# Linear attention followed by a gated feed-forward block: new row layout, k maximum as a factor on v, new load order

## The chip, the cores and the metric

The kernel runs on one core of one Trainium2 chip. The metric is the time of one execution in microseconds (us) on the device. A run counts as slow when it is over 1.5% above the fastest of the same kernel.

The engines in the profile: PE is the tensor engine, PEld its weight loads, DVE the vector engine, ACT the scalar engine, POOL the GpSimd engine, SP the sync engine. SPq and POOLq mark the issuing of DMA transfers. PSUM is the memory that the matmuls of these kernels write to, SBUF the one that holds all other tiles. The buffers of a tile in a pool are called its ring. L230 is line 230 of the kernel in question, so the same work has different line numbers in different kernels.

## The reference

```python
# q, k, v: (8, 8, 576, 64) = batch, head, row, feature; omega: (128, 64)
def phi(x):                                    # x = q * scale or k * scale
    proj = einsum('bhsd,md->bhsm', x, omega)
    h = proj - sum(x * x, -1, keepdims) / 2
    h = h - max(h, -1, keepdims)
    return exp(h) / sqrt(m)
kv  = einsum('bhsm,bhsd->bhmd', k_p, v);  z = sum(k_p, axis=2)
num = einsum('bhsm,bhmd->bhsd', q_p, kv); den = einsum('bhsm,bhm->bhs', q_p, z) + 1e-6
x   = (num / den) as (4608, 512)               # 8 heads side by side
out = (gelu(x @ w_gate) * (x @ w_val)) @ w_out # (512, 1536), (512, 1536), (1536, 512)
```

Factors that are constant in a row of q cancel in num / den, so the kernel needs no maximum for q (the 1e-6 aside). For k, exp(proj − max) can be written as exp(proj) · exp(−max): the second factor belongs to a row of k and may as well be multiplied onto that row of v (and onto the 1 that sums up z).

## The kernel before

A *batch* is one of the 8 batch entries, with 576 tokens. The FFN works on 9 tiles of 512 tokens. Attention for batch t+1 is woven into the FFN of tile t, so that the tensor engine fills the waits of attention with FFN matmuls. For batches 2 to 7, k and q are transposed by DMA, and so is the attention's result x; batches 0 and 1 use the tensor engine for it.

```python
SM = 512; R = 4; SR = S - SM        # rows 0..511 of a head: s = 4p + r; 64 rows left over
work = ctx.enter_context(tc.tile_pool(name="work", bufs=2))
att  = ctx.enter_context(tc.tile_pool(name="att", bufs=2, space=PSUM))
mo   = ctx.enter_context(tc.tile_pool(name="mo", bufs=4, space=PSUM))
# ... loads: k, q of a batch in three pieces each on the GpSimd queue, v in three on the sync queue ...
def k_feat(ps, dst, n):             # for each PSUM tile of keys
    nmax = work.tile([P, n, 1], F32, name="nmax", bufs=4)
    nc.vector.reduce_max(nmax, ps, axis=AX, negate=True)
    kd = work.tile([P, n, M], F32, name="kd", bufs=5)
    nc.vector.tensor_add(kd, ps, nmax.broadcast_to((P, n, M)))
    nc.scalar.activation(dst, kd, func=Exp)
# ... pk in four tiles and a left-over one; q features; kz = k_p^T [v, 1] ...
for rp in range(2):
    x_sb = work.tile([P, 2, d_model], BF16, name="x_sb")       # the pool's 2 buffers
    for r2 in range(2):
        nd = att_tile([P, 2, 512], F32, "nd")
        # ... 8 matmuls into nd, reciprocal of the denominators ...
        nc.vector.tensor_mul(x_sb[:, r2]..., ndv[:, :, :, :D], iden.broadcast_to(...))
    if on_dma:                                                 # batches 2 to 7
        for r2 in range(2):
            put_x_dma(tok + (2 * rp + r2) * P, x_sb[:, r2], P) # DMA transposes x_sb -> xT
        continue
# ... the 64 left-over rows go another way, through PSUM ...
def gate_val(t):
    for jf in range(N_DFF):                                    # 12 times
        g_ps = mo.tile([P, T_TOK], F32, name="g_ps", tag="mo") # 4 matmuls of 512 columns
        nc.scalar.activation(g_gelu, g_ps, func=Gelu)
        v_ps = mo.tile([P, T_TOK], F32, name="v_ps", tag="mo") # 4 matmuls
        nc.vector.tensor_mul(gated[:, jf, :], g_gelu, v_ps)
```

The softmax here doesn't subtract the row's maximum and nothing guards it: scores larger than these inputs give would overflow.

Of the kernel before, what the change touches and what calls it, by code (L numbers as in the profile page):

```python
# [10 lines left out]
F32 = mybir.dt.float32  # L11
# [4 lines left out]
def kernel(  # L16
# [29 lines left out]
    SM = 512  # L46
    R = 4
    SR = S - SM
# [5 lines left out]
    AX = mybir.AxisListType.X  # L54

# [8 lines left out]


    def load_kq(b):
        tiles = []
        for src, nm in ((k, "k"), (q, "q")):
            both = ld.tile([P, 2 * H + 2, P], BF16, name=f"{nm}_in")
            main = both[:, :2 * H].rearrange("p (h c) x -> p h (c x)", h=H)  # L70
            rest = both[:, 2 * H:].rearrange("p c (j d) -> p (c j) d", j=2)
            nc.gpsimd.dma_start(  # L72
                out=main,
                in_=src[b, :, :SM, :].rearrange("h (p r) d -> p h (r d)", r=R))
            for e in range(2):
                hs = src[b].rearrange("(j e) s d -> e j s d", e=2)[e] if nm == "k" \
                    else src[b, 4 * e:4 * e + 4]
                nc.gpsimd.dma_start(
                    out=rest[e * SR:(e + 1) * SR],
                    in_=hs[:, SM:, :].rearrange("j s d -> s j d"))  # L80
            tiles += [both, main, rest]
        return tiles

    v_ext = [singles.tile([P, H, R, DP1], BF16, name=f"v_ext{i}") for i in range(2)]

    v_rbd = [singles.tile([P, 4, 2, DP1], BF16, name=f"v_rbd{i}") for i in range(2)]

    for i in range(2):
        nc.vector.memset(v_rbd[i], 0.0)
        nc.vector.memset(v_ext[i][:, :, :, D:DP1], 1.0)  # L90
        for e in range(2):
            nc.vector.memset(v_rbd[i][e * SR:(e + 1) * SR, :, e, D:DP1], 1.0)

    def load_v(b):
        vf = ld.tile([P, H, R * D], F32, name="vf", bufs=1)
        vrf = ld.tile([P, 4, D], F32, name="vrf", bufs=1)
        nc.sync.dma_start(
            out=vf, in_=v[b, :, :SM, :].rearrange("h (p r) d -> p h (r d)", r=R))
        for e in range(2):
            nc.sync.dma_start(  # L100
                out=vrf[e * SR:(e + 1) * SR],
                in_=v[b].rearrange("(j e) s d -> e j s d", e=2)[e, :, SM:, :]
                    .rearrange("j s d -> s j d"))
        ve, vr = v_ext[b % 2], v_rbd[b % 2]
        nc.gpsimd.tensor_copy(ve[:, :, :, :D],
                              vf.rearrange("p h (r d) -> p h r d", r=R))
        for e in range(2):
            sl = slice(e * SR, (e + 1) * SR)
            nc.gpsimd.tensor_copy(vr[sl, :, e, :D], vrf[sl])
        return ve, vr  # L110

    omega_f = singles.tile([M, D], F32)
    nc.sync.dma_start(out=omega_f, in_=omega)
    kq = {0: load_kq(0)}
    vx = {0: load_v(0)}

    ident = singles.tile([P, P], BF16)
    make_identity(nc, ident)
    omega_bf = singles.tile([M, D], BF16)
    nc.vector.tensor_scalar_mul(omega_bf, omega_f, scale)  # L120
    omegaT_ps = att_tile([D, M], BF16, "omegaT_ps")
    nc.tensor.transpose(omegaT_ps, omega_bf, ident)
    omegaT2 = singles.tile([2 * D, M], BF16)
    omega2T = singles.tile([2 * D, 2 * M], BF16)
    nc.vector.memset(omega2T, 0.0)
    for e in range(2):
        sl = slice(e * D, (e + 1) * D)
        nc.vector.tensor_copy(omegaT2[sl], omegaT_ps)
        nc.vector.tensor_copy(omega2T[sl, e * M:(e + 1) * M], omegaT_ps)
# [12 lines left out]

    load_gv(0)
    kq[1] = load_kq(1)
    vx[1] = load_v(1)
    load_gv(1)
    load_gv(2)
    for c in range(3):
        nc.gpsimd.dma_start(out=w_out_sb[:, 4 * c:4 * c + 4, :], in_=wo[:, 4 * c:4 * c + 4, :])


    x_tiles = {}

    def put_x(c0, src):

        n, done = src.shape[2], 0
        while done < n:
            t, c = divmod(c0 + done, T_TOK)
            m = min(n - done, T_TOK - c)
            if t not in x_tiles:  # L160
                x_tiles[t] = work.tile([P, N_DM, T_TOK], BF16, name="xT", bufs=3)
            nc.vector.tensor_copy(x_tiles[t][:, :, c:c + m], src[:, :, done:done + m])
            done += m

    def put_x_dma(c0, src, n):

        done = 0
        while done < n:
            t, c = divmod(c0 + done, T_TOK)
            m = min(n - done, T_TOK - c)  # L170
            if t not in x_tiles:
                x_tiles[t] = work.tile([P, N_DM, T_TOK], BF16, name="xT", bufs=3)
            nc.sync.dma_start_transpose(out=x_tiles[t][:, :, c:c + m],
                                        in_=src[done:done + m, :])
            done += m


    def transpose_dma(both, nm):
        t_sb = work.tile([P, 2 * H + 2, P], BF16, name=f"{nm}T", tag="kqT")
        nc.sync.dma_start_transpose(out=t_sb, in_=both.rearrange("p c x -> p (c x)"))  # L180
        return t_sb

    def transpose_main(src, nm):
        t_ps = att_tile([P, 2 * H, P], BF16, f"{nm}T_ps")
        for h in range(H):
            for rp in range(2):
                nc.tensor.transpose(t_ps[:, 2 * h + rp, :],  # L187
                                    src[:, h, rp * P:(rp + 1) * P], ident)
        t_sb = work.tile([P, 2 * H + 2, P], BF16, name=f"{nm}T", tag="kqT")[:, :2 * H]
        nc.vector.tensor_copy(t_sb, t_ps)  # L190
        return t_sb

    def attention(b):
        k_both, k_in, k_rest, q_both, q_in, q_rest = kq.pop(b)
        ve, vr = vx.pop(b)
        on_dma = b > 1
        if on_dma:
            kT = transpose_dma(k_both, "k")
            qT = transpose_dma(q_both, "q")
            krT, qrT = kT[:, 2 * H:], qT[:, 2 * H:]  # L200
        else:
            kT = transpose_main(k_in, "k")
            rT_ps = att_tile([P, 4, P], BF16, "rT_ps")
            for i, src in enumerate((k_rest, q_rest)):
                for jj in range(2):
                    nc.tensor.transpose(
                        rT_ps[:, 2 * i + jj, :],
                        src[:, 2 * jj:2 * jj + 2, :].rearrange("p j d -> p (j d)"), ident)
            rT = work.tile([P, 4, P], BF16, name="rT")
            nc.vector.tensor_copy(rT, rT_ps)  # L210
            krT, qrT = rT[:, :2], rT[:, 2:]


        k_p = work.tile([P, H, R, M], BF16, name="k_p")
        k_pr = work.tile([P, 4, M], BF16, name="k_pr")

        def k_feat(ps, dst, n):
            nmax = work.tile([P, n, 1], F32, name="nmax", bufs=4)
            nc.vector.reduce_max(nmax, ps, axis=AX, negate=True)  # L219
            kd = work.tile([P, n, M], F32, name="kd", bufs=5)  # L220
            nc.vector.tensor_add(kd, ps, nmax.broadcast_to((P, n, M)))  # L221
            nc.scalar.activation(dst, kd, func=Exp)  # L222

        for hp in range(H // 2):
            pk = att_tile([P, 8, M], F32, "pk")
            for i in range(4):
                nc.tensor.matmul(pk[:, 2 * i:2 * i + 2, :], kT[:, 4 * hp + i, :], omega2T)  # L227
            k_feat(pk, k_p[:, 2 * hp:2 * hp + 2].rearrange("p h r m -> p (h r) m"), 8)
        pkr = att_tile([P, 4, M], F32, "pkr")
        for jj in range(2):  # L230
            nc.tensor.matmul(pkr[:, 2 * jj:2 * jj + 2, :], krT[:, jj, :], omega2T)
        k_feat(pkr, k_pr, 4)


        if not on_dma:
            qT = transpose_main(q_in, "q")
        q_pT = work.tile([P, H // 2, 2, 4, P], BF16, name="q_pT")
        q_pTr = work.tile([P, 2, 2, P], BF16, name="q_pTr")
        for hp in range(H // 2):
            pq = att_tile([P, 2, 512], F32, "pq")  # L240
            for r2 in range(2):
                sl = slice(r2 * D, (r2 + 1) * D)
                nc.tensor.matmul(pq[:, r2, :], omegaT2[sl],  # L243
                                 qT[sl, 4 * hp:4 * hp + 4, :])
            nc.scalar.activation(  # L245
                q_pT[:, hp].rearrange("m a c p -> m a (c p)"), pq, func=Exp)
        pqr = att_tile([P, 2, 512], F32, "pqr")
        for j2 in range(2):
            sl = slice(j2 * D, (j2 + 1) * D)
            nc.tensor.matmul(pqr[:, j2, :256], omegaT2[sl], qrT[sl])  # L250
        nc.scalar.activation(q_pTr.rearrange("m a c p -> m a (c p)"), pqr[:, :, :256], func=Exp)


# [152 lines left out]
```

## Time and profile before

| what | value |
|---|---|
| median of 3 runs | 399.51 us (398.19 to 399.78) |
| profiled span | 398.3 us, mean granted clock 0.977 |
| PE / DVE / ACT / POOL busy | 355.4 / 224.2 / 154.6 / 63.0 us |
| start of the stage of batch 2 | 91.65 us |
| one stage from there (one batch's attention with one tile's FFN) | 38.2 us four times and 38.4 once; then 115.4 us to the end |

The start of a stage is read from the scalar engine. Exp and Gelu use different tables, and the timeline shows each change of table (1.28 us); the change to Exp (L222 before) stands right before a batch's first exponentials of k. I use these moments as stage marks.

The page's slices of the kernel before (40 equal slices; each digit is the busy share in tenths, or the granted clock in tenths) with the chain that ended last (by engine):

```profile
PE   0446756999999999999999999999999999999995
PEclk9999985899999999999999999999999999999999
PE 80%; DVE 9%; DMA 4%; issue 2%; ACT 2%; POOL 1%; SPq 0%; DVEq 0%; POOLq 0%
```

PE is half idle in the first 70 us and busy at 90% or more from then on. The busy table of one stage (window, its length, then busy time and instruction count of each engine, granted clock, DMA share, GB/s) says the same by number:

```profile
91.65:129.84 38.19, 37.98 (x247) 18.07 (x250) 25.05 (x38) 18.73 (x24) 6.99 (x9) 1.00 0.79 135
```

PE is busy 37.98 of 38.19 us at full clock, DVE only 25.05. In the start, the timeline of the first keys shows a chain on DVE (start, duration, engine, line, instruction; in brackets the idle time before it and what ended it):

```profile
17.34 1.91 PE L227 MATMUL pk<-omega2T,kT 128*128 128x256 bf16 x8
18.44 2.36 DVE L219 TENSOR_REDUCE nmax<-pk 128x8 f32<-128x1024 f32 x2 [0.43 <-PE pk L227]
20.71 2.35 DVE L221 TENSOR_TENSOR kd<-pk,nmax 128x1024 f32<-128x1024 f32 x2
...
21.99 2.17 PE L227 MATMUL pk<-omega2T,kT 128*128 128x256 bf16 x8 [2.73 <-DVE kd L221]
```

Two key tiles take two maxima and two adds, 4.7 us in all, and PE reuses the first one's PSUM tile only after its add, at 21.99. The last view of before is of the tile `x_sb` in one stage.

```profile
L281 DVE TENSOR_TENSOR x_sb<-nd,iden x4: 680/688/692, 111.1 to 113.8; 128x512 bf16<-128x512 f32 x4
L173 SPq DMA_TRANSPOSE xT<-x_sb x4: 1226/1332/1455, 119.3 to 123.6; - x4
DMA to landing us min/median/max: 5.9/7.2/7.6
```

The four products are written from 111.1 to 113.8 us. Their transposes are issued only from 119.3 to 123.6, and land 5.9 to 7.6 us after issue. They are late, and nothing waits for them here.

### The profile page before, as it was taken

The page shows a single profiled execution, that of the slowest core. Times are in us where ns is not written, and L with a number is a line of the kernel's source. Part 1 is how long each engine was busy: PE and PEld are TensorE (multiplying, and loading weights), DVE is VectorE, ACT ScalarE, POOL GpSimd, SP SyncE. Part 2 cuts the span into 40 slices and gives each one's busy share as a digit, 9 for nine tenths or more (in the row PEclk, how much of TensorE's full clock was granted, in tenths as well). Part 3 has the DMA queues.
Part 4 walks back from the last instruction along what each step waited for, and adds up shares of the span by engine and source line. Part 5 has one row for each costly group of instructions (what it writes and reads, how often), then busy time and mean ns, then how long its engine had stood idle before and what let it go on. Part 6 is the DMA issues. An engine that isn't in the chain of part 4 may idle for free.

```text
span 398.3 us, 5658 instructions
## 1 busy us (share of the span) xinstructions
PE 355.4 (89%) x2212; PEld 174.2 (44%) x2249; DVE 224.2 (56%) x345; ACT 154.6 (39%) x202; POOL 63.0 (16%) x87
## 2 busy tenths in 40 slices
PE   0446756999999999999999999999999999999995
PEld 0323523545444544444444444454535444444442
DVE  1392593748574956495559546864776423433332
ACT  1044027234833482447335633653464312311310
POOL 7563422600222041104100200000000000000000
PEclk9999985899999999999999999999999999999999
DMA  9999999980799089909992820371022012002004
GB/s 179 234 213 219 206 232 154 192 157 0 142 158 209 8 144 225 150 11 189 167 150 47 185 49 1 70 176 35 0 88 58 16 33 72 2 27 81 0 10 95
DMA packets 89626, 43.65 MB, mean 110 GB/s; under 512 B 55808, under 2 KB 84992, under 8 KB 89600
## 3 DMA queue, kind: packets, MB, share of 16 engines
q1 hardware_dynamic: 59504, 29.14, 34.2%
q0 software_dynamic: 30096, 14.16, 28.1%
q8 instruction: 17, 0.28, 0.3%
q14 instruction: 9, 0.07, 0.1%
HBM read 37.78 MB, written 9.44 MB: 119 GB/s over the span
## 4 chain that ended last, share of the span: by engine, by line
PE 80%; DVE 9%; DMA 4%; issue 2%; ACT 2%; POOL 1%; SPq 0%; DVEq 0%; POOLq 0%
PE g_ps L327 23%; PE v_ps L333 23%; PE o_ps L357 21%; DVE nmax L219 3%; DMA q_in<-in_q_dram 3%; DVE kd L221 3%; PE pk L227 3%; PE nd L276 2%; PE kz_ps L261 2%; PE pq L243 2%; ACT q_pT L245 2%; DMA out_dram<-o_sb 1%; PE qT_ps L187 1%; DVE x_sb L281 1%; DVE o_sb L360 1%
## 5 line engine op out<-in xcount | busy, mean ns | idle before, releaser
L335 DVE TENSOR_TENSOR gated<-g_gelu,v_ps 128x512 bf16<-128x512 bf16 x108 | 73.8, 683 | 86.2 <-PE v_ps L333 80.9
L330 ACT ACTIVATE g_gelu<-g_ps 128x512 bf16<-128x512 f32 x108 | 64.4, 597 | 141.2 <-PE g_ps L327 133.1
L327 PE MATMUL g_ps<-xT,w_gate_sb 128*128 128x512 bf16 x419 | 116.0, 382 | 1.5 <-issue 0.4
L333 PE MATMUL v_ps<-xT,w_val_sb 128*128 128x512 bf16 x417 | 109.9, 379 | 1.2 <-issue 0.6
L357 PE MATMUL o_ps<-w_out_sb,gated 128*128 128x512 bf16 x423 | 98.6, 379 | 0.4
L222 ACT ACTIVATE k_p<-kd 128x1024 bf16<-128x1024 f32 x32 | 33.8, 1057 | 77.6 <-DVE kd L221 76.4
L333 PEld LDWEIGHTS <-w_val_sb 128*128 128x128 bf16 x432 | 41.3, 98 | 46.9 <-issue 0.5
L357 PEld LDWEIGHTS <-gated 128*128 128x128 bf16 x432 | 41.3, 98 | 45.7 <-issue 2.7
L327 PEld LDWEIGHTS <-w_gate_sb 128*128 128x128 bf16 x432 | 40.3, 98 | 44.6 <-issue 3.7
L360 DVE COPY o_sb<-o_ps 128x512 f32<-128x512 f32 x36 | 24.2, 686 | 40.8 <-PE o_ps L357 21.2
L219 DVE TENSOR_REDUCE nmax<-pk 128x8 f32<-128x1024 f32 x32 | 37.6, 1216 | 1.1 <-PE pk L227 1.1
L221 DVE TENSOR_TENSOR kd<-pk,nmax 128x1024 f32<-128x1024 f32 x32 | 37.5, 1215 | 0.0
L245 ACT ACTIVATE q_pT<-pq 128x1024 bf16<-128x1024 f32 x32 | 30.0, 1023 | 3.9 <-PE pq L243 3.9
L227 PE MATMUL pk<-omega2T,kT 128*128 128x256 bf16 x128 | 20.0, 294 | 5.0 <-DVE kd L221 4.9
L281 DVE TENSOR_TENSOR x_sb<-nd,iden 128x512 bf16<-128x512 f32 x32 | 21.5, 688 | 0.4
L72 POOL DMA_DIRECT2D k_in<-in_k_dram x8 | 7.3, 914 | 80.1 <-DMA kT<-k_in 79.1
L227 PEld LDWEIGHTS <-kT 128*128 128x128 bf16 x128 | 11.8, 103 | 14.4 <-DVE kd L221 11.4
L243 PE MATMUL pq<-qT,omegaT_109 64*128 64x512 bf16 x64 | 13.9, 440 | 4.6 <-DVE qT L190 2.6
L265 DVE CAST kz<-kz_ps 128x520 bf16<-128x520 f32 x8 | 5.6, 698 | 20.0 <-PE kz_ps L261 20.0
L276 PEld LDWEIGHTS <-q_pT 128*128 128x128 bf16 x256 | 11.3, 104 | 9.2 <-DVE x_sb L281 3.8
L276 PE MATMUL nd<-kz,q_pT 128*128 128x65 bf16 x256 | 13.4, 203 | 1.6 <-DVE kz L265 1.2
L72 POOL DMA_DIRECT2D q_in<-in_q_dram x8 | 7.2, 906 | 36.0 <-DMA qT<-q_in 16.4
(69 smaller groups left out, 192.1 us busy)
## 6 DMA issues: line engine op xcount, KB each, us to landing
vf<-in_v_dram SPq DMA_DIRECT2D x8, 1024.0 KB, 8.7
out_dram<-o_sb SPq DMA_DIRECT2D x40, 128.0 KB, 2.4
k_in<-in_k_dram POOLq DMA_DIRECT2D x8, 512.0 KB, 9.1
q_in<-in_q_dram POOLq DMA_DIRECT2D x8, 512.0 KB, 10.6
out_dram<-o_sb SPq DMA_DIRECT2D x16, 256.0 KB, 2.9
w_gate_sb<-in_moe_w_gate_dram POOLq DMA_DIRECT2D x3, 512.0 KB, 15.0
w_val_sb<-in_moe_w_val_dram POOLq DMA_DIRECT2D x3, 512.0 KB, 14.3
w_out_sb<-in_moe_w_out_dram POOLq DMA_DIRECT2D x3, 512.0 KB, 18.9
```

The source lines that it names most:

```text
L219: nc.vector.reduce_max(nmax, ps, axis=AX, negate=True)
L221: nc.vector.tensor_add(kd, ps, nmax.broadcast_to((P, n, M)))
L222: nc.scalar.activation(dst, kd, func=Exp)
L227: nc.tensor.matmul(pk[:, 2 * i:2 * i + 2, :], kT[:, 4 * hp + i, :], omega2T)
L245: nc.scalar.activation(q_pT[:, hp].rearrange("m a c p -> m a (c p)"), pq, func=Exp)
L276: nc.tensor.matmul(nd[:, h // 4, (h % 4) * DP1:(h % 4 + 1) * DP1], q_pT[:, h // 2, r2, 2 * (h % 2) + rp, :], kz_h(h))
L327: nc.tensor.matmul(g_ps, w_gate_sb[:, jm, fs], xT[:, jm, :], start=(jm == 0), stop=(jm == N_DM - 1))
L330: nc.scalar.activation(g_gelu, g_ps, func=Gelu)
L333: nc.tensor.matmul(v_ps, w_val_sb[:, jm, fs], xT[:, jm, :], start=(jm == 0), stop=(jm == N_DM - 1))
L335: nc.vector.tensor_mul(gated[:, jf, :], g_gelu, v_ps)
L357: nc.tensor.matmul(o_ps, gated[:, jf, qq * P:(qq + 1) * P], w_out_sb[:, jf, :], start=(jf == 0), stop=(jf == N_DFF - 1))
L360: nc.vector.tensor_copy(o_sb, o_ps)
```

## The change

The intent: a head's 576 rows are taken as s = 9p + r on 64 partitions, with an even and an odd head of a pair on the two halves of the partitions. So 576 = 64 · 9 leaves no rows over, and the extra tiles, loads and matmuls for them go away. The maximum of k becomes a factor `wk` on v, which removes the add `kd`. Loads are ordered by need. The core of the diff, with cuts marked:

```diff
-    SM = 512
-    R = 4
-    SR = S - SM
+    SP = 64
+    R = S // SP
 ...
-    load_gv(0)
-    kq[1] = load_kq(1)
-    vx[1] = load_v(1)
-    load_gv(1)
+    load_kq("k", 0, parts=2)
+    load_kq("q", 0)
+    load_v(0)
+    load_kq("k", 1)
+    load_kq("q", 1)
+    load_gv(0)
+    load_gv(1)
+    load_v(1)
 ...
-            nc.vector.reduce_max(nmax, ps, axis=AX, negate=True)
-            nc.vector.tensor_add(kd, ps, nmax.broadcast_to((P, n, M)))
-            nc.scalar.activation(dst, kd, func=Exp)
+            nc.scalar.activation(k_p[:, :, i0:i0 + n, :], pk[:, :, :n, :], func=Exp)
+            nc.vector.reduce_max(nmax[:, :, i0:i0 + n], pk[:, :, :n, :], axis=AX, negate=True)
 ...
+            if i0 == 0:
+                nc.scalar.activation(wk, nmax, func=Exp)
+            nc.vector.tensor_mul(vev[:, isl, :, :D], vfv[:, isl], wkv[...].broadcast_to(...))
+            nc.vector.tensor_copy(vev[:, isl, :, D], wkv[:, isl])
 ...  kz: per head 9 matmuls on 64 rows, the two heads of a pair on the two halves
-        for rp in range(2):
-            x_sb = work.tile([P, 2, d_model], BF16, name="x_sb")
-            for r2 in range(2):
+        for r0 in range(0, R, 2):
 ...
+            x_sb = work.tile([P, d_model], BF16, name="x_sb", bufs=3)
             nc.vector.tensor_mul(x_sb..., ndv[:, :, :, :D], iden...)
```

## The prediction

> **What bounds the kernel now.** From about 92 us on, the page's slices show PE at 90% or more. In the timeline the first pk matmuls of consecutive batches start at 91.9, 130.1, 168.3, ... 321.3 us: a period of 38.2 us. Its 144 FFN matmuls, 0.216 us apart, take 31.1; the other 7.1 us are attention work on PE. PE alone bounds this part; DVE has 25 busy us of 38. Before 70 us PE is half idle: attention(0) and attention(1) run one after the other as chains of latencies. Keys wait for the last q load (17.05); then each 128x1024 tile costs a 1.22 us maximum and a 1.22 us add on DVE before its 1.06 us exp. x of batch 0 is ready at 45.6, attention(1) starts at 47.0, and because ACT is in program order the first gelu waits until 69.8.
>
> **Removed.** The add kd (5.5 us of DVE per batch), left-over tiles, POOL casts of v, small loads, the wait of the first keys for q. **Added.** v times the factor: two 128x1152 fp32 products, estimated at 1.3 us each from the add's 1.22 for 1024; q's exps in halves (ten, about 0.5 us apart); 416 more matmuls. **Moved.** k and q of batch 1 load before the weights; row runs grow from 1 to 2.3 KB. Total bytes stay.
>
> **Critical path, start.** q(0) still lands near 15 to 17 us because v(0) and v(1) load beside it, but keys are done by then. I estimate x(0) near 35 instead of 45.6, and attention(1) about 18 instead of 21.5 us long (its later key tiles stand behind eight cold FFN matmuls). First gelu: about 54. Gate(0) then takes 22 us as before, so pk of batch 2 starts near 77 instead of 91.9, if its transposed keys are there; they landed at 72 before. Gain: about 15 us.
>
> **Critical path, steady part.** kz becomes 72 matmuls on 64 rows, pk 36. The Trainium skill (TensorE: Matmul & The Clock Gate, "Packing small matmuls") says that matmuls in different row groups run concurrently; this trace agrees: two pq matmuls (64 rows each, 512 columns) span 0.39 us against 0.38 for one. So a kz pair should cost about one old 30 ns matmul, and pk falls from 1.9 to about 1.1 us. But entering and leaving the 64-row form costs about 0.1 us each way (pq pair to next o_ps: 0.32 us for 0.216 of columns); pk in four pieces and kz add about five such round trips, 1 us. Waits of kz for the last exps or v's product may add 0.3. Net: period +0.3 us (-0.4 to +1.0), times 6: +2 us. The last 77 us (FFN only) stay.
>
> **Prediction: 386.5 us**, range 377 to 394. Faster by over 2%: 0.80; within 2%: 0.19; slower by over 2%: 0.01.
>
> **What would show it.** Right: first gelu at 50 to 58 us; first pk of batch 2 at 72 to 81; later periods 37.8 to 39.2 us; 77 us after the last one. Wrong: a period above 39.5 (pairs not concurrent, or PE waiting for ACT or DVE inside the projection); pk of batch 2 waiting for transposed keys; first gelu after 60.
>
> **What would make it wrong.** kz pairs running one after the other (+1 to 2 us a period); q(0) landing after 18 us, since both v loads now go first; the cold PE clock lengthening the start; or loads landing faster with longer rows (x(0) near 30 us, total near 380).

## More of the kernel before

A batch writes two `x_sb` tiles of two blocks of 128 rows, and the pool has two buffers. So a tile is written again only one batch later.

## The result and the profile after

| | before | after |
|---|---|---|
| median of 4 runs | 399.25 us (398.19 to 399.78) | 433.56 us (432.3 to 438.15) |
| ratio of fast runs | | 1.0884, 95% interval 1.0798 to 1.097: slower |
| profiled span, mean granted clock | 398.3 us, 0.977 | 430.6 us, 0.947 |
| first gelu table load | 68.53 | 58.67 |
| start of the stage of batch 2 | 91.65 | 82.26 |
| the five stages from there | 38.2 four times, 38.4 | 50.25, 50.49, 51.74, 40.68, 38.00 |
| from the last mark to the end | 115.4 | 117.2 |

Ratios are the mean time of one kernel's fast runs over that of the other's of the same rounds, so they are not quite the ratio of the medians.

The account from these marks: start −9.4, five stages +39.9 (231.2 against 191.2), rest +1.8, together +32.3 us, which is the difference of the spans. The start did gain. The steady part, which was to cost 2 us, lost 40.

The slices and the chain of after:

```profile
PE   1466779997299946999189998999999899999995
PEclk9999859999599996999879999999999999999999
PE 75%; DMA 11%; DVE 4%; ACT 3%; SPq 3%; issue 1%; POOL 0%; DVEq 0%; POOLq 0%
```

In the row of PE there are holes (2; 4 and 6; 1 and 8; a last shallow 8) at regular distance, with a lower granted clock behind them. The chain has 11% DMA instead of 4%; by line, 8.7% of the span is the transfer `xT<-x_sb`, which the chain of before does not name. The waits of the whole execution (engine, line, what it waited for: us in total, times, longest):

```profile
DVE x_sb L230 <- DMA xT<-x_sb: 44.1, 11, 10.7
PE g_ps L256 <- DVE gated L264: 36.0, 5, 11.7
```

The corresponding waits of before have no line of DVE or PE that waits for this DMA. The timeline of one hole (lines between left out):

```profile
93.94 0.74 POOL L84 DMA_DIRECT2D k_in<-in_k_dram  x1 [27.26 <-DMA kT<-k_in]
94.36 6.63 SPq L146 DMA_TRANSPOSE qT<-q_in  x1
...
97.85 0.69 DVE L230 TENSOR_TENSOR x_sb<-nd,iden 128x512 bf16<-128x512 f32 x1
...
102.32 1.58 SPq L90 DMA_DIRECT2D vf<-in_v_dram  x1
...
104.00 2.62 SPq L235 DMA_TRANSPOSE xT<-x_sb  x2
...
110.21 0.69 DVE L230 TENSOR_TENSOR x_sb<-nd,iden 128x512 bf16<-128x512 f32 x1 [8.62 <-DMA xT<-x_sb]
...
113.94 0.68 DVE L230 TENSOR_TENSOR x_sb<-nd,iden 64x512 bf16<-64x512 f32 x1 [3.04 <-DMA xT<-x_sb]
114.55 1.86 DVE L264 TENSOR_TENSOR gated<-g_gelu,v_ps 128x512 bf16<-128x512 bf16 x3
115.27 1.87 PE L256 MATMUL g_ps<-xT,w_gate_sb 128*128 128x512 bf16 x4 [10.36 <-DVE gated L264]
...
116.93 1.91 PE L262 MATMUL v_ps<-xT,w_val_sb 128*128 128x512 bf16 x4
...
118.64 1.14 PE L256 MATMUL g_ps<-xT,w_gate_sb 128*128 128x512 bf16 x4
```

Read it from below. Three products v_ps stood unread in the ring of four `mo` PSUM tiles, and PE waited 10.36 us for DVE's first `gated` before it wrote the next `g_ps`. DVE takes its instructions in order, and the five `x_sb` products of the batch stand before the twelve `gated`: the first `gated` had its inputs at 102.1 us and ran at 114.55. The fourth product waited 8.62 us because its buffer is that of the first, whose transpose had not landed; the fifth waited 3.04 us for the second's. The transposes were late because the sync engine's queue was held: the transpose of q took 6.63 us to issue, beside the load of k, and stores and the load of v stood before the transposes of x. When PE began again it was slow: the four matmuls at 115.27 and the next four started about 0.42 us apart, twice the 0.216 of full clock. The busy tables of the whole stage and of 115.27 to 118.64 give the granted clock, 0.90 and 0.50, and for the second nine matmuls in 3.37 us:

```profile
82.26:132.51 50.25, 39.88 (x303) 17.61 (x302) 23.25 (x36) 19.01 (x30) 1.48 (x2) 0.90 0.52 104
115.27:118.64 3.37, 3.37 (x9) 1.16 (x9) 1.14 (x2) 0.60 (x1) 0.00 (x0) 0.50 0.11 19
```

The Trainium skill ("TensorE: Matmul & The Clock Gate", "Part 1: The HAM clock gate") says that an idle window of about 3.4 us drops the array to half its clock, and that about 3.4 us of work lifts it again. This trace agrees: 10.36 us of idle, then half rate for 3.37 us.

Idle time and half rate together give the length of the stages. Without a hole a stage is 37.98 us (shown below), so the first has 12.27 us too many: 10.4 of idle, and most of the rest from half rate, since half of 3.4 us is 1.7.

The same run holds a comparison in itself, because the last stages have fewer loads. `x_sb` in the first stage shown, and in the stage from 275.42, which loads nothing:

```profile
L235 SPq DMA_TRANSPOSE xT<-x_sb x5: 1171/1212/1310, 104.0 to 114.7; - x5
  DMA xT<-x_sb: 11.7, 2
DMA to landing us min/median/max: 2.3/6.1/8.5
...
L235 SPq DMA_TRANSPOSE xT<-x_sb x5: 1192/1222/1256, 291.7 to 298.3; - x5
  DMA xT<-x_sb: 0.8, 2
DMA to landing us min/median/max: 2.3/2.4/2.5
```

With loads beside them the transposes land 6.1 us after issue in the median and DVE loses 11.7 us; without loads they land after 2.4 us and DVE loses 0.8. The stage in between, from 234.74, still loads v but no k and q; it waits 3.9 us and is 40.68 us long. So one has a dose and a response: loads make the transposes late, and the ring of three makes lateness into a wait.

### The profile page after: what moved, and what is told of

It is laid out like the page before. It is cut to its first block, busy times and chain, and to the rows that moved or that the text cites. A ratio compares the mean times of both kernels' runs of the same rounds, so it can differ in the third digit from the quotient of the medians.

```text
span 430.6 us, 6524 instructions
## 1 busy us (share of the span) xinstructions
PE 362.0 (84%) x2673; PEld 168.9 (39%) x2673; DVE 208.9 (49%) x326; ACT 156.5 (36%) x250; POOL 20.0 (5%) x32
## 4 chain that ended last, share of the span: by engine, by line
PE 75%; DMA 11%; DVE 4%; ACT 3%; SPq 3%; issue 1%; POOL 0%; DVEq 0%; POOLq 0%
PE o_ps L280 23%; PE g_ps L256 21%; PE v_ps L262 20%; DMA xT<-x_sb 9%; PE pk L170 3%; PE pq L183 2%; DMA k_in<-in_k_dram 2%; PE nd L223 2%; ACT q_pT L185 2%; PE kz_ps L210 2%; DVE nmax L172 1%; SPq L235 1%; PE qT_ps L152 1%; PE xt_ps L240 1%; DVE x_sb L230 1%
## 5 line engine op out<-in xcount | busy, mean ns | idle before, releaser
L171 ACT ACTIVATE k_p<-pk 128x1024 bf16<-128x1024 f32 (+1 forms) x40 | 36.7, 937 | 43.9 <-PE pk L170 43.3
L230 DVE TENSOR_TENSOR x_sb<-nd,iden 128x512 bf16<-128x512 f32 (+1 forms) x40 | 27.5, 689 | 44.8 <-DMA xT<-x_sb 44.1
L172 DVE TENSOR_REDUCE nmax<-pk 128x8 f32<-128x1024 f32 (+1 forms) x40 | 42.6, 1114 | 12.4 <-ACT k_p L171 12.4
L185 ACT ACTIVATE q_pT<-pq 128x512 bf16<-128x512 f32 (+1 forms) x80 | 37.4, 586 | 9.8 <-PE pq L183 9.8
L199 DVE TENSOR_TENSOR v_ext<-vf,wk 128x1152 bf16<-128x1152 f32 x16 | 21.7, 1357 | 5.7 <-ACT wk L189 5.7
L170 PE MATMUL pk<-omegaT_106,kT 64*128 64x128 bf16 x288 | 14.9, 229 | 5.5 <-DVE nmax L172 5.2
L183 PE MATMUL pq<-qT,omegaT_106 64*128 64x512 bf16 (+1 forms) x80 | 16.7, 411 | 2.9 <-ACT q_pT L185 2.2
L223 PEld LDWEIGHTS <-q_pT 128*128 128x128 bf16 (+1 forms) x320 | 13.8, 106 | 10.3 <-DVE x_sb L230 4.0
L223 PE MATMUL nd<-kz,q_pT 128*128 128x65 bf16 (+1 forms) x320 | 17.1, 202 | 0.8 <-DVE kz L214 0.8
L210 PE MATMUL kz_ps<-v_ext,k_p 64*128 64x65 bf16 x576 | 12.3, 203 | 1.2 <-ACT q_pT L185 1.2
## 6 DMA issues: line engine op xcount, KB each, us to landing
k_in<-in_k_dram POOLq DMA_DIRECT2D x7, 576.0 KB, 10.2
```

What stands on the lines that cost most here:

```text
L170: nc.tensor.matmul(pk[:, a, i, :], kT[sl, i0 + i, :], omegaT2[sl])
L171: nc.scalar.activation(k_p[:, :, i0:i0 + n, :], pk[:, :, :n, :], func=Exp)
L172: nc.vector.reduce_max(nmax[:, :, i0:i0 + n], pk[:, :, :n, :], axis=AX, negate=True)
L185: nc.scalar.activation(q_pTv[:, a, i0:i0 + n], pq[:, a, :n, :].rearrange("m i (e p) -> m i e p", e=2), func=Exp)
L210: nc.tensor.matmul(kz_ps[:, e, j * DP1:(j + 1) * DP1], k_p[sl, u % 2, u // 2, :], ve[sl, u, :], start=(r == 0), stop=(r == R - 1))
L223: nc.tensor.matmul(nd[:n, h // 4, (h % 4) * DP1:(h % 4 + 1) * DP1], q_pT[:, e, u:u + nr, :].rearrange("m r p -> m (r p)"), kz[:, e, j * DP ...
```

## The experiments

The theory: *the ring is too short*. Three `x_sb` buffers for five tiles make DVE wait for transposes in mid-batch, and PE for DVE. Rivals: *the queue is too full* (the v load on the sync queue, with its longer rows, is what makes transposes late, and moving it would cure it); *the new layout costs it* (more small matmuls, changes of form on PE, waits inside the attention).

### Six x tiles

```diff
-            x_sb = work.tile([P, d_model], BF16, name="x_sb", bufs=3)
+            x_sb = work.tile([P, d_model], BF16, name="x_sb", bufs=6)
```

> The changed kernel with six x_sb buffers instead of three, nothing else. Theory A (the ring of three x_sb tiles is too short: the fourth product of a batch waits on VectorE for the DMA transposes of the first, and the gated products behind it starve PE): no wait of x_sb for the transposes, all periods 38 to 39 us, start as in the changed kernel (first pk of batch 2 near 82.5), total 388 to 393 us. Theory B (the extra matmuls and the switches to 64 rows make the projection stage longer): periods stay near 50, total above 420.

Measured: 389.91 us (388.42 to 390.81), ratio to before 0.9749 (0.9715 to 0.9783), faster. One number in the kernel moves the time by 43.7 us. The busy table of a stage, and `x_sb` in the stage that answers to the one above:

```profile
120.38:158.36 37.98, 37.38 (x298) 17.15 (x302) 23.33 (x36) 19.00 (x31) 1.48 (x2) 1.00 0.83 138
...
L235 SPq DMA_TRANSPOSE xT<-x_sb x5: 1213/1251/1552, 104.0 to 110.7; - x5
DMA to landing us min/median/max: 4.5/6.0/8.2
```

The transposes are as late as before (first issue at 104.0, landing 6.0 us later in the median), but no instruction waits for them. The stage is 37.98 us long with PE busy for 37.38. So the new layout, with the factor on v, does not cost the stage anything: that rival is out. It even gains 0.2 us a stage over the 38.2 of before.

### Four and five x tiles

The same line with `bufs=4` and `bufs=5`.

> The changed kernel with four x_sb buffers. Theory A: only the fifth, 64-row tile of a batch waits, and for the first transpose instead of the second, so the three long periods fall from 50.5 to about 46.5 us and the total to about 415 to 422. If three against five tiles were not the matter, it stays at 433.

> Five single x tiles. Theory (the loss is a tile's reuse inside one batch, since a batch has five tiles and the fourth and fifth wait for the transposes of the first and second): with five no tile is reused inside a batch, the next batch's reuse comes over 30 us later; periods 38.0 us, no wait for the transpose before an x product, 389 to 391.5 us as with six. Rival (lateness of transposes as such, at any depth): something between the four's 421 and the six's 390, about 400.

Measured with four: 420.9 us (418.43 to 424.5), ratio 1.0535 (1.0457 to 1.0613), slower. DVE waits 32.6 us for the transposes, 5 times. Its stages are 46.4, 47.3, 48.9, 40.0 and 38.0 us. Now only the fifth tile reuses a buffer of its own batch, that of the first tile, but the fifth product still stands before the `gated` products, and one long wait is enough.

Measured with five: 388.91 us (388.2 to 389.19), ratio 0.9725 (0.9691 to 0.976). The waits have no line for the transposes any more, and the stages are 37.98 us. The step from four to five is the whole of the loss that was left, and six adds nothing. The expectations of all three runs were met or nearly so (with four, a stage took up to 48.9 us where about 46.5 was expected). The number that matters is therefore the count of tiles in a batch: what hurts is reuse inside a batch.

### The same ring shortage in the kernel before

```diff
-            x_sb = work.tile([P, 2, d_model], BF16, name="x_sb")
+            x_sb = work.tile([P, 2, d_model], BF16, name="x_sb", bufs=1)
```

> The kernel before with one x_sb buffer (two tiles of 128 rows) instead of two (four tiles). Theory A: the same stall appears in the kernel before: the third product of a batch waits for the transposes of the first two, periods with loads grow from 38.2 to 46 to 52 us, total 425 to 445. If the ring is not the cause, it stays at 399.

Measured: 446.49 us (445.06 to 447.93), ratio 1.1161 (1.1113 to 1.121). Old layout, old loads, and a ring that is one tile short: the loss is 46.5 us against 43.7 in the new layout. Its timeline and waits:

```profile
118.66 12.37 SPq L173 DMA_TRANSPOSE xT<-x_sb  x4
...
127.81 1.29 DVE L281 TENSOR_TENSOR x_sb<-nd,iden 128x512 bf16<-128x512 f32 x2 [11.11 <-DMA xT<-x_sb]
...
DVE x_sb L281 <- DMA xT<-x_sb: 39.2, 6, 11.6
PE ndr L298 <- DVE x_sb L281: 37.7, 6, 11.2
```

Here PE waits inside the attention (`ndr`), not at `g_ps`, but the cause in front of it is the same line. Its stages are 50.4, 49.9, 51.7, 43.2 and 39.2 us, nearly those of after. The expectation was met; the time is just above its 445 us.

### v loads moved to the other issuing engine, three x tiles kept

```diff
-        nc.sync.dma_start(out=t, in_=rows_of(v, b))
+        nc.gpsimd.dma_start(out=t, in_=rows_of(v, b))
```

> The changed kernel, three x_sb buffers kept, v loaded from the GpSimd queue behind k and q, so that no v load stands on the SyncE queue in front of the x transposes. Rival C (it is the 1.2 MB v load in front of the transposes that makes them late): long periods fall to 39 or 40, total under 400. Theory A (anything that makes the transposes late is felt, and the k and q loads still compete): long periods fall by 2 or 3 us only, total 420 to 430. Beside that the first keys should land sooner, since v(0) and v(1) no longer compete with them: first key transposes at 6 to 8 us instead of 9.7, first pk of batch 2 about 3 to 5 us earlier than 82.4.

Measured: 441.68 us for all four runs; the three fast ones took 436.48 to 442.2 us, the slow one 448.54. Ratio of the fast runs 1.1005 (1.0929 to 1.1081), slower. Taking the v load out of the sync queue did not help; it is no better than the 433.56 of after. The first stages became longer (53.3, 57.4, 51.7, 43.7 and 38.0 us), where one theory expected 39 or 40 and the other 2 or 3 us less than 50.5: both missed. The start gained what was expected (stage mark 77.48 instead of 82.26). The timeline of one stage and the waits:

```profile
89.08 0.74 POOL L84 DMA_DIRECT2D k_in<-in_k_dram  x1 [20.99 <-DMA kT<-k_in]
89.58 12.49 SPq L146 DMA_TRANSPOSE qT<-q_in  x1
90.19 0.76 POOL L90 DMA_DIRECT2D vf<-in_v_dram  x1 [0.37 <-DVE v_ext L201]
...
103.44 3.84 SPq L235 DMA_TRANSPOSE xT<-x_sb  x2
...
DVE x_sb L230 <- DMA xT<-x_sb: 57.5, 8, 18.7
```

The v load now starts 12 us earlier (7 us earlier in its stage, since the stage itself begins 4.8 us sooner), right behind the load of k, and the transpose of q runs beside both: 12.49 us to issue it, against 6.63 beside k alone and 1.83 in the stage without loads. The queue in front of the transposes of x got shorter by one entry and longer in time. The Trainium skill ("DMA: Bandwidth & Descriptors", "Issuing engines are not separate DMA queues") says that transfers from all issuing engines run on the same 16 DMA engines and interleave. The run agrees.

### The start: load order, and the place of the maximum

With the ring mended, the first stage mark stood at 82.39 us where I had predicted 77. Two parts of the change could be tried alone, both with six x tiles. First the old order of loads:

```diff
-    load_kq("k", 0, parts=2)
+    load_kq("k", 0)
     load_kq("q", 0)
     load_v(0)
+    load_gv(0)
     load_kq("k", 1)
     load_kq("q", 1)
-    load_gv(0)
-    load_gv(1)
     load_v(1)
+    load_gv(1)
```

> Six x_sb buffers, but the loads in the order of the kernel before (k and q of batch 1 behind the first third of the weights, k of batch 0 in one piece). If the new load order buys the earlier start, first pk of batch 2 moves from 82.4 back toward 88 to 92 us and the total to 395 or more. If the start is bound by the chain of work of the two first batches (keys of batch 1 landed long before they were needed), nothing moves: 82 to 83 us, total 389 to 392.

Measured: 389.66 us (389.25 to 390.64), ratio 0.9767 (0.9727 to 0.9806), unclear against the 2% mark but no different from the 389.91 of six tiles; the stage mark at 82.77. Nothing moved. The order of loads, as the change has it, is worth nothing that the times can show. The 0.4 us of the mark is within the scatter: the runs with four, five and six tiles, whose loads are the same, have it at 80.54, 81.78 and 82.39, and this run's profile had a granted clock of 0.62 from 14 to 40 us where that of six tiles had 1.00.

Second, the maximum read from the exponentials in SBUF instead of from PSUM. Since exp is monotone, the reciprocal of the largest exponential is the factor:

```diff
-            nc.vector.reduce_max(nmax[:, :, i0:i0 + n], pk[:, :, :n, :], axis=AX, negate=True)
+            nc.vector.reduce_max(nmax[:, :, i0:i0 + n], k_p[:, :, i0:i0 + n, :], axis=AX)
-                nc.scalar.activation(wk, nmax, func=Exp)
+                nc.vector.reciprocal(wk, nmax)
```

> Six x_sb buffers, and the maximum taken by VectorE from the exponentials k_p in SBUF (factor = reciprocal of the maximum) instead of from pk in PSUM. If the start is 5 us later than I forecast because exp and maximum of a key tile run one behind the other on the same PSUM tile and hold it 2.3 us, pk of batch 0 and 1 no longer waits for the maximum, each of the two attentions shrinks by about 3 us, first pk of batch 2 near 77, total 383 to 386. If the cold PE clock or the x part is to blame, it stays at 82 and 389. Periods stay at 38.0.

Measured: 389.15 us (388.96 to 389.83), ratio 0.9753 (0.9716 to 0.9791). The total is that of the six tiles, but it is made up in another way. The stage mark is at 77.84, 4.6 us earlier and near the 77 expected, and the stages are 38.6 us instead of 37.98, in all five that the marks give; so the expected 38.0 and 383 to 386 us were missed. The first keys of after, and then of this run:

```profile
13.98 0.61 PE L170 MATMUL pk<-omegaT_106,kT 64*128 64x128 bf16 x8
14.63 1.94 ACT L171 ACTIVATE k_p<-pk 128x1024 bf16<-128x1024 f32 x2 [12.61 <-PE pk L170]
...
15.69 2.35 DVE L172 TENSOR_REDUCE nmax<-pk 128x8 f32<-128x1024 f32 x2 [0.84 <-ACT k_p L171]
16.96 0.61 PE L170 MATMUL pk<-omegaT_106,kT 64*128 64x128 bf16 x8 [1.46 <-DVE nmax L172]
```

```profile
15.40 4.26 ACT L171 ACTIVATE k_p<-pk 128x1024 bf16<-128x1024 f32 x5 [13.38 <-PE pk L170]
...
16.47 0.61 PE L170 MATMUL pk<-omegaT,kT 64*128 64x128 bf16 x8 [0.20 <-ACT k_p L171]
17.39 0.61 PE L170 MATMUL pk<-omegaT,kT 64*128 64x128 bf16 x8 [0.30 <-ACT k_p L171]
```

In after, exp and maximum of a key tile run one after the other on the same PSUM tile, so PE's third tile waits for DVE. In this run PE's tiles come 0.9 us apart and the five exps run without a gap. The Trainium skill ("PSUM — Partial Sum Buffer", "PSUM bank collisions raise a hardware error") says that two engines may not access one bank at once, reads included. The trace agrees with such an order: in after, DVE waits 16 times for the exp before it takes the maximum, 12.4 us in all. It need not be the whole of the 4.6 us: 3.2 of them are there at the change to the gelu table (55.51 against 58.72), and the other 1.3 come in the FFN of tile 0, where the granted clock was 0.93 against 0.88. Why the stages became 38.6 us long is visible in part: with another instruction order on PE, the matmuls of kz wait 0.4 us for `v_ext`.

### v of the first two batches on the other queue as well

To the run before, for batches 0 and 1 alone:

```diff
-        nc.sync.dma_start(out=t, in_=rows_of(v, b))
+        (nc.gpsimd if b < 2 else nc.sync).dma_start(out=t, in_=rows_of(v, b))
```

> As the run with the maximum from SBUF, and v of batches 0 and 1 loaded from the GpSimd queue in its place between the keys. First keys land 4 to 5 us sooner (seen with v on that queue), so first pk of batch 2 near 72, periods 38.0, total 378 to 382: faster than both kernels.

Measured: 385.65 us (384.13 to 386.33), ratio 0.9668 (0.9624 to 0.9713). The stage mark moves to 72.58, as expected. On the sync queue the loads of v(0) and v(1) went out with the first keys and shared the DMA engines with them; the two halves of k(0) were used by PE at 9.73 and 12.91 us. On the GpSimd queue v stands behind k and q: in this run the same two points are 5.21 and 8.46 us. This run and the one with all v loads moved suggest that moving an issue helps where it puts a transfer *later*, not because it puts it on another engine; no run delays v on the sync queue alone. The stages are still 38.6 us, so the expected 38.0 and 378 to 382 us were missed.

### The subtraction put back

With six x tiles and the new layout, the maximum is subtracted again (`kd`), and v is only cast:

```diff
-            nc.scalar.activation(k_p[:, :, i0:i0 + n, :], pk[:, :, :n, :], func=Exp)
             nc.vector.reduce_max(nmax[:, :, i0:i0 + n], pk[:, :, :n, :], axis=AX, negate=True)
+            kd = work.tile([P, 2, n, M], F32, name="kd", bufs=4)
+            nc.vector.tensor_add(kd, pk[:, :, :n, :], nmax[...].broadcast_to(...))
+            nc.scalar.activation(k_p[:, :, i0:i0 + n, :], kd, func=Exp)
 ...
-            nc.vector.tensor_mul(vev[:, isl, :, :D], vfv[:, isl], wkv[...].broadcast_to(...))
-            nc.vector.tensor_copy(vev[:, isl, :, D], wkv[:, isl])
+            nc.vector.tensor_copy(vev[:, isl, :, :D], vfv[:, isl])
+            nc.vector.memset(vev[:, isl, :, D], 1.0)
```

> Six x_sb buffers, but the subtraction of the maximum before exp put back (kd on VectorE; v copied, ones in the last column). It undoes one part of the change. If leaving out kd is what makes the start earlier, first pk of batch 2 goes back by 2 to 3 us for each of the two first batches or more, to 86 to 90 us; the periods stay at 38.0 to 38.3, since VectorE has slack there; total 393 to 398.

Measured: 408.85 us (408.13 to 409.66), ratio 1.0244 (1.0204 to 1.0285), which is slower than before. The stage mark is at 90.46 instead of 82.39, and a stage is 39.8 us instead of 37.98. The expectation (stages of 38.0 to 38.3, 393 to 398 us) counted on slack on DVE and was missed. The busy table and a piece of the timeline of one stage:

```profile
130.27:170.09 39.82, 37.94 (x298) 17.12 (x302) 26.33 (x41) 19.05 (x30) 1.48 (x2) 1.00 0.69 132
...
149.18 0.69 DVE L261 TENSOR_TENSOR gated<-g_gelu,v_ps 128x512 bf16<-128x512 bf16 x1 [3.69 <-ACT g_gelu L256]
149.79 0.69 DVE L211 CAST kz<-kz_ps 128x520 bf16<-128x520 f32 x1
...
150.54 0.66 PE L220 MATMUL nd<-kz,q_pT 128*128 128x65 bf16 x16 [1.40 <-DVE kz L211]
```

DVE is busy 26.33 of 39.82 us, far from full, and still makes PE wait: the cast of kz stands behind a `gated` that waits for its gelu. So the layout without the factor on v brings nothing here; the factor is what makes it pay, about 8 us of the start and 1.8 us a stage. The comparison isn't quite with the old treatment, since the cast of v is on DVE here and was on POOL before. Whether a better order on DVE would take back the 1.8 us I did not try.

### Together

Six x tiles; maximum from SBUF and v on the GpSimd queue for batches 0 and 1 only; batches 2 to 7 as with six tiles:

```diff
-        nc.sync.dma_start(out=t, in_=rows_of(v, b))
+        (nc.gpsimd if b < 2 else nc.sync).dma_start(out=t, in_=rows_of(v, b))
 ...
-            nc.vector.reduce_max(nmax[:, :, i0:i0 + n], pk[:, :, :n, :], axis=AX, negate=True)
+            if on_dma:
+                nc.vector.reduce_max(nmax[:, :, i0:i0 + n], pk[:, :, :n, :], axis=AX, negate=True)
+            else:
+                nc.vector.reduce_max(nmax[:, :, i0:i0 + n], k_p[:, :, i0:i0 + n, :], axis=AX)
 ...
-                nc.scalar.activation(wk, nmax, func=Exp)
+                if on_dma:
+                    nc.scalar.activation(wk, nmax, func=Exp)
+                else:
+                    nc.vector.reciprocal(wk, nmax)
 ...
-            x_sb = work.tile([P, d_model], BF16, name="x_sb", bufs=3)
+            x_sb = work.tile([P, d_model], BF16, name="x_sb", bufs=6)
```

> Six single x tiles, and in batches 0 and 1 alone the largest of k taken from the copy of k in SBUF and v loaded from the other issuing engine; batches 2 to 7 as in the run with six tiles. Theory (start and steady part add): first k product of batch 2 near 72.6 us as in the run g3_best, periods of 38.0 us as in e1_xsb6 instead of 38.6, so 378 to 382.5 us. Rival (the 38.6 us period comes from how the shorter start shifts the queues, not from the order on the tensor engine): periods stay 38.6 and the time stays at 385 to 386.5.

Measured: 381.24 us (380.66 to 382.01, 5 runs), ratio to before 0.9539 (0.9513 to 0.9565). This beats both kernels. The stage mark is at 73.13, and the stages are 37.98 us (row of PE in the slices, and the busy table of one stage):

```profile
PE   1756679999999999999999999999999999999994
73.13:111.11 37.98, 37.38 (x298) 17.18 (x302) 23.33 (x36) 19.01 (x31) 2.22 (x3) 1.00 0.77 153
```

Gain of the start and length of the stage add up, as the theory had it. The 38.6 us of the two runs before came with the other treatment of the maximum in the later batches, not with the earlier start.

## Why the prediction was wrong, and where it was right

**The step that failed** is the steady part: "Net: period +0.3 us (-0.4 to +1.0), times 6: +2 us". The first three stages became 12.3 to 13.8 us longer than the 37.98 us that they take with a longer ring. The prediction counted what PE and DVE have to *do* ("PE alone bounds this part; DVE has 25 busy us of 38") and did not count the buffers through which they hand work on. The diff had `bufs=3` in plain sight, against five tiles a batch, and the trace of before showed that the transposes which free these buffers are issued 8 us after the first product and land 6 to 8 us later. Both facts were to be had. The prediction named one wait for a DMA, that of pk of batch 2 for its transposed keys; it did not name the ring, nor the wait of an x product for a transpose. That the ring is the cause is shown from both sides: with five or six tiles the loss is gone, and with a shorter ring the kernel before has it.

**Right, with the ring out of the way:** the cost of the attention on PE. The prediction's 38.5 us for a stage (+0.3) was 37.98 (-0.2), inside its range of -0.4 to +1.0. "a kz pair should cost about one old 30 ns matmul": the 72 kz matmuls span 1.33 us in the trace of after (from 95.02), and the 36 matmuls of before took 1.42 (107.93 to 109.35), so the pairs do run side by side, as the page cited in the prediction says.

**Right in kind, too large in size:** the start. "x(0) near 35", "first gelu: about 54" and "pk of batch 2 starts near 77" were 40 (the first FFN matmuls at 39.88), 59.97 and 82.41; so 9.4 of the 15 us came. Two terms were found. The prediction did not reckon with the exp and the maximum of a key tile taking turns on the PSUM tile; taking the maximum elsewhere is worth 4.6 us. And v(0), v(1) were said not to matter because "keys are done by then"; they slow the very first keys, and putting them behind is worth 5.3 us more (77.84 to 72.58). Together that is more than the miss of about 5.5 us, so something else in the estimate was too slow; what, was not looked for. The new order of loads was worth nothing. That six tiles came out at 389.91 us, inside the range of 377 to 394, is in part luck: about half of the late start was made up by stages 0.5 us shorter than predicted.

**Right:** the last part without attention stayed. It is 115.4 us from the last mark both in before and with six tiles; after has 117.2, in which waits for `x_sb` of the last batch (3.6 us on DVE) may have a share. One slip in reading: the last value that the prediction lists as a start of pk, 321.3, is the end of the sixth stage; there is no pk there. It did not enter the sum.

**What stays open:** why a stage takes 38.6 us when the maximum is read from SBUF in every batch. The wait of kz explains 0.4 us; that the order on PE differs was seen, but no run separates the two.

## What to carry to other kernels

When a change alters how many tiles of a kind are written before the next long wait, count them against the ring, and look up in the trace how late the reader of the oldest one finishes. A late transfer that nobody waits for is harmless until a buffer makes somebody wait, and a wait in front of an in-order engine stops everything behind it. A regular hole in the row of the busiest engine is the sign; the Trainium skill says so too ("Perfetto Trace Analysis", "Optimization Strategy": a gap that keeps repeating can mean that there is no room for the next tile), and here the gaps of 10.4, 9.9 and 11.7 us went away with two more tiles.

## What the Trainium skill lacked or had wrong

- "DMA: Bandwidth & Descriptors" gives an effective bandwidth for DMA transposes ("Latency and other measured facts": 261 GB/s, more if contiguous), but no time for one that runs beside loads. Here the transpose of q (128x2304 in 2-byte elements, 0.59 MB) landed 3.9 and 5.5 us after issue in the two stages where no load ran beside it, 9.4 to 10.2 us beside the load of k (three stages), and 18.9 to 23.8 us beside the loads of k and v (three stages of the run with moved v loads).
- The same page says that spreading DMAs over issuing engines saves only sequencer time. What it lacks is how long the sync engine itself is held for the issue of a transpose beside loads: 1.8 us, 6.6 to 7.3 us and 8.1 to 12.5 us in those three cases, and everything queued behind it waits.
- "Perfetto Trace Analysis" names too few buffers as a possible cause of repeating gaps, and has one look for what the waiting engine waits on. What it lacks is that this can take a second step: here the line of the idle engine named only DVE (36.0 us of PE), and the waits of the engine *in front of* it named the buffer (44.1 us of DVE for the transfer out of `x_sb`).
